# Copies of finished attention results asked for behind all second products of their group

## Chip, cores and metric

The kernel runs on one core of one Trainium2 chip. The metric is the device time of one execution in microseconds (us); the median of three runs before the change is 1055.65 us (1052.11, 1055.65 and 1055.78).

## What is computed

A sigmoid attention over 4 batches and 12 heads, sequence 448, head width 64, followed by two feed-forward layers over the 1792 tokens (widths 768 and 2048), the second with a rational activation. Only the attention is touched:

```python
scores = scale * np.matmul(q, k.transpose(0, 1, 3, 2)) - np.log(S)
attn = 1.0 / (1.0 + np.exp(-scores))
return np.matmul(attn, v)
...
h = x @ w_in;  g = h * sigmoid(h);          x = g @ w_out
h = x @ w_in2; g = P(h) / (Q(h) + 1e-6);  out = g @ w_out2
```

There is no normalisation over the keys, so a result is a plain sum over chunks of keys.

## The kernel before

**Tiling.** Two heads of a batch make a pair; there are 24 pairs (i = 0 to 23). The keys of a pair are cut into chunks of 128, three full ones (c = 0, 1, 2), and the remaining 64 keys of an even pair and of the odd pair behind it share a fourth chunk (c = 3, `LAST`), the even pair's in one half of the partitions and the odd pair's in the other. A **unit** (i, c) is one such chunk, and two pairs make seven units: (e,0) to (e,3), (e+1,0) to (e+1,2). In all there are 84.

**A unit's work.** `attn_QK` (L382) forms the scores on TensorE: three passes (high by high, low key by high query, high key by low query) for two heads, 6 products, or 12 for a shared chunk, where the second six are the next pair's. They go into one of three PSUM buffers called `pair`. `attn_S` (L396) lets ScalarE take the sigmoid from there into SBUF. `attn_AV` (L405) forms the **second products**, sigmoids by values, 4 per unit (8 of half the height for a shared chunk). They add up in `hb`, one PSUM tile of two halves, where even pairs use half 0 and odd pairs half 1. When the last chunk of a pair has been added (the shared one for an even pair, c = 2 for an odd one), `attn_E` copies that half out with VectorE: for the first two batches into `xk` (L420), for the last two into `sb` (L423) with a DMA to DRAM behind it on SyncE's queue (L424).

**Order of the work.** The program's order is written out by hand, and each engine goes through its own part of it in that order. The loop over `groups()` takes three units per turn (the very first three are taken as two and one) and gives, in this order: VectorE's transposition of the queries of a new pair (`attn_X`, L359); the first products of the three units; their sigmoids; TensorE's transposition of the new pair's keys into a `pair` buffer (`attn_T`, L354); the second products of the *previous* turn's three units; and then `attn_C`, which splits the new pair's keys and queries into high and low parts: two ScalarE copies (L365) and two VectorE subtractions (L367), keys first, from the `pair` buffer and from `xq`. Behind that come operand splits for the next layer (`operands0`: L440, L445 and GpSimd's subtractions L482), weight conversions (L237 to L245) and loads.

**Where results get finished.** Six pairs make seven turns (a *block*, four in all), numbered 0 to 6 here. Six of the seven turns finish one pair each, and so copy it once: turns 2 and 3 with the first of their three units, turns 4 and 5 with the second, turns 6 and the next block's 0 with the third. Before the change `attn_E` is called inside `attn_AV`, straight behind the unit that finishes the pair.

```python
for u, p_ in [(u, attn_QK(*u)) for u in units]:
    attn_S(*u, p_)
p = attn_T(new) if new < NPT else None
for u in waiting:
    attn_AV(*u)
waiting = units
if p is not None:
    attn_C(new, *p)
```

**Buffers that matter here.** `pair` is a ring of three: `attn_T` takes the one that the first unit's sigmoid gave back, and the third unit of the next turn gets that same buffer once `attn_C` has read it. `hb` is allocated as one tile, and its two halves are views of it.

Of the kernel before, what the change touches and what calls it, by code (L numbers as in the profile page):

```python
# [47 lines left out]
def attention_moe_moe(ctx: ExitStack, tc: tile.TileContext, q, k, v, w_in1, w_out1, w_in2, w_out2, a, b2, out):  # L48
# [134 lines left out]
    def conv_outs():  # L183
        for do in outs:
            do()
        outs.clear()
# [65 lines left out]
    def conv_rest():  # L252
        for do in halves:
            do()
        halves.clear()
# [15 lines left out]
    def rest_of(i):  # L271
        return HI if i % 2 else LO
# [17 lines left out]
    def load_q(i):  # L290
        if i >= NPT:
            return
        b, hp = divmod(i, NP)
        t = qs[i] = ld_p[0].tile([P, S], F32, tag="qs", name=f"qs_{i}", bufs=3)
        for part in range(2 * D // SQ):
            j, e0 = divmod(part * SQ, D)
            (nc.scalar if i == 0 and part % 2 else nc.sync).dma_start(
                out=t[part * SQ : (part + 1) * SQ, :].rearrange("l (c d) -> l c d", d=SQ),
                in_=q[b, 2 * hp + j, :, e0 : e0 + SQ].rearrange("(c l) d -> l c d", l=SQ),
            )  # L300
# [3 lines left out]
    def mix(i):  # L304
        if i >= NPT:
            return
        t = ks.pop(i)
        u = mixed[i] = ld_p[0].tile([P, 2 * NCH * D], F32, tag="km", name=f"km_{i}", bufs=2)
        dst, src = u.rearrange("p (c h d) -> p h c d", c=NCH, h=2), t.rearrange("p h (c d) -> p h c d", c=NCH)
        if i:  # L310
            nc.gpsimd.tensor_copy(dst, src)
            return
        for h, eng in enumerate((nc.vector, nc.gpsimd)):
            eng.tensor_copy(dst[:, h], src[:, h])
# [34 lines left out]
    def attn_T(i, p=None):  # L349
        t = mixed.pop(i)  # L350
        pk = p if p is not None else pairs.get()
        o = p if p is not None else pk[:, 0, :]
        for c in range(NCH):
            nc.tensor.transpose(o[:, c * P : (c + 1) * P], t[:, c * P : (c + 1) * P], ident)  # L354
        return p, pk, o

    def attn_X(i):
        x = xq[i] = ld_p[0].tile([P, S], F32, tag="xq", name=f"xq_{i}", bufs=1)
        nc.vector.transpose(x, qs.pop(i))  # L359

    def attn_C(i, p, pk, o):
        k_, q_ = st["k", i], st["q", i] = kst.get(), qst.get()
        both = ((k_, o[:, :BK]), (q_, xq.pop(i)))
        for x, src in both:
            nc.scalar.copy(x[:, 0, :], src)  # L365
        for x, src in both:
            nc.vector.tensor_tensor(out=x[:, 1, :], in0=src, in1=x[:, 0, :].bitcast(F32), op=ALU.subtract)  # L367
        if p is None:
            pairs.put(pk)
# [3 lines left out]
    def attn_QK(i, c):  # L373
        p = pairs.get()
        parts = [(i, ((0, 0), (1, 0), (0, 1)))]
        if c == LAST:
            parts.append((i + 1, parts[0][1]))
        turns = [(i_, n) for i_, passes in parts for n in passes]
        for n, (i_, (a_, b_)) in enumerate(turns):
            K, Q = st["k", i_], st["q", i_]  # L380
            for j in range(2):
                nc.tensor.matmul(  # L382
                    p[:, j, :S],
                    K[rows[j], a_, c * P : (c + 1) * P],
                    Q[rows[j], b_, :],
                    start=(n == 0),
                    stop=(n == len(turns) - 1),
                )
        if c == (LAST if i % 2 == 0 else LAST - 1):
            kst.put(st.pop(("k", i)))  # L390
            qst.put(st.pop(("q", i)))
        return p

    def attn_S(i, c, p):
        t = f2.get()
        nc.scalar.activation(t, p[:, :, :S], AF.Sigmoid, bias=nls, scale=QKSCALE)  # L396
        pairs.put(p)
        at[i, c] = t

    def attn_AV(i, c):  # L400
        t = at.pop((i, c))
        for i_ in (i,) if c < LAST else (i, i + 1):
            part = slice(0, P) if c < LAST else rest_of(i_)
            for j in range(2):
                nc.tensor.matmul(  # L405
                    hb[i_ % 2][j * D : (j + 1) * D, :S],
                    vs[i_][part, j, c * D : (c + 1) * D],
                    t[part, j],
                    start=(c == (LAST if i_ % 2 else 0)),
                    stop=(c == (LAST - 1 if i_ % 2 else LAST)),  # L410
                )
        f2.put(t)
        if c == (LAST - 1 if i % 2 else LAST):
            attn_E(i)

    def attn_E(i):
        b, hp = divmod(i, NP)
        del vs[i]
        if b < 2:
            nc.vector.tensor_copy(xk[b * KD + hp], hb[i % 2][:, :S])  # L420
            return
        t = xio.get()
        nc.vector.tensor_copy(t[:, :S], hb[i % 2][:, :S])  # L423
        nc.sync.dma_start(out=xs[0][hp][:, b * S : (b + 1) * S], in_=t[:, :S])  # L424
        xio.put(t)
# [17 lines left out]
    def flush():  # L443
        for src, h, lo in lows:
            nc.vector.tensor_tensor(out=lo, in0=src, in1=h.bitcast(F32), op=ALU.subtract)  # L445
        lows.clear()
# [155 lines left out]
    def prep_ij(g):  # L602
        if g < NGR:
            split_later(wf[g % 2][0], wr[0], wr[1])
# [440 lines left out]
    with tc.manual_schedule():  # L1045
# [33 lines left out]
        def groups():  # L1079
            units = [(i, c) for e in range(0, NPT, 2) for i, c in (*((e, c) for c in range(NCH)), *((e + 1, c) for c in range(LAST)))]  # L1080
            yield (0,), units[:2], 1
            yield (1,), units[2:3], NPT
            at_ = 3
            for e in range(0, NPT, 6):
                n = 2 * e
                for j, (first, size) in enumerate(((0, 2), (2, 1), (3, 2), (5, 2), (7, 1), (8, 2), (10, 2))):
                    if e == 0 and j == 0:
                        continue
                    yield tuple(range(n + first, n + first + size)), units[at_ : at_ + 3], e + 1 + j if j else NPT
                    at_ += 3  # L1090
            assert at_ == len(units)

        begun = 0
        for steps, units, new in groups():
            conv_outs()
            if 0 in steps:
                mix(2)
            for n in steps:
                if n % 2:
                    mix(n // 2 + 3)  # L1100
            if new < NPT:
                attn_X(new)
            for u, p_ in [(u, attn_QK(*u)) for u in units]:
                attn_S(*u, p_)
            p = attn_T(new) if new < NPT else None
            for u in waiting:
                attn_AV(*u)
            waiting = units
            if p is not None:
                attn_C(new, *p)  # L1110
            flush()
            if new < NPT:
                load_q(new + 3)
            conv_rest()
            while begun < (steps[-1] + 1 - 14) * 3 // 4:
                flush()
                next(first_ops, None)
                begun += 1
            for n in steps:
                i, h = divmod(n, 2)  # L1120
                if h == 0:
                    load_k(i + 5)
                at_half = n - 2 * NPT
                if n % 4 == 1:
                    load_v(i + 2)
                    load_v(i + 3)
                if at_half == -8:
                    load_w1(0)
                    load_w1(1)
                if at_half == -5:  # L1130
                    xk_s.close()
                    wr_p, wr_s = opened("wr")
                    wr_p.tile([P, PAD], F32, tag="wrpad", name="wrpad")
                    wr.extend(fixed("wr", 4, [P, DM], F32R, wr_p))
                    wq.extend(fixed("wq", 6, [P, HM], F32R, wr_p))
                    prep_ij(0)
                    sums_12(0)
                if at_half == -3:
                    prep_s12(0)
                if at_half == -1:  # L1140
                    prep_a22(0)
                if n == 0:
                    conv_load()
                if n == 3:
                    conv_load()
                if n == 4:
                    coefficients()
                if n == 12:
                    coefficients_abs()
                if n in CONVS:  # L1150
                    conv(True)
        for _ in first_ops:
            pass
        for u in waiting:
            attn_AV(*u)
        flush()
        bits.put(more_bits)
        ld_s.close()
# [254 lines left out]
        for n in range(HN):  # L1413
# [32 lines left out]
            if n > 3 * HF:  # L1446
                i = n - 3 * HF - 1
# [85 lines left out]
```

## Time and profile before

| what | value |
|---|---|
| median of three runs | 1055.65 us |
| the profiled execution, its own time | 1055.2 us |
| its span in the trace | 1053.4 us |
| TensorE products / weight loads busy | 1028.2 us (98%) / 894.6 us (85%) |
| VectorE, ScalarE, GpSimd busy | 689.3, 653.9, 269.9 us |
| attention, from the first products to the next layer's first | about 7 to 177 us |
| second products L405 | 384, 75.5 us busy, 12.8 us idle ahead of them |

The span is what the trace covers; the time of the execution is 1.8 us longer. "Idle before" is time in which an engine did nothing just ahead of an instruction, with what released it. A product's row is longer than its place in the pipeline, since products overlap; the distance between two starts says what a piece of work costs TensorE. The groups of products in the timeline are merged, so a row "x12" has twelve of them from the start shown.

### The profile page before, as it was taken

Reading aid. Unit: us, or ns where it says so; the run is one execution under the profiler, and the core shown is the slowest. Engines: PE = TensorE matmul, PEld = TensorE weight load, DVE = VectorE, ACT = ScalarE, POOL = GpSimd, SP = SyncE. Lnnn points to the kernel's source line nnn. Section 1 sums busy time; section 2 is a strip of 40 time slices with the busy share of each in tenths; the row PEclk is TensorE's granted clock in tenths of the full one; section 3 lists DMA queues with packets and bytes.
Section 4 is the critical chain, followed back from the end, with each engine's and each line's share of the span. In section 5 each row is a group of like instructions: output and inputs, shape, how many; then the busy total and the mean of one; then the engine's idle time right before and its main releaser. Section 6 shows DMA issues by size and latency. Waiting matters only on the chain.

```text
span 1053.4 us, 15903 instructions
## 1 busy us (share of the span) xinstructions
PE 1028.2 (98%) x5568; PEld 894.6 (85%) x5568; DVE 689.3 (65%) x982; ACT 653.9 (62%) x971; POOL 269.9 (26%) x242
## 2 busy tenths in 40 slices
PE   8999899999999999999999999999999999999998
PEld 5454455899999988899998888888999999999998
DVE  3456544888877748354545628989898977655761
ACT  6677665777676658355545648677777866354430
POOL 4234340000000000000000036579877932310000
PEclk9999999999999999999999999999999999999999
DMA  9866672788777758398979753567678968986641
GB/s 184 184 148 137 143 203 83 249 279 290 247 260 266 268 187 323 106 356 299 369 298 388 307 165 105 200 242 232 218 252 292 314 210 285 333 300 200 206 162 53
DMA packets 182352, 246.15 MB, mean 234 GB/s; under 512 B 57152, under 2 KB 136640, under 8 KB 182272
## 3 DMA queue, kind: packets, MB, share of 16 engines
q1 hardware_dynamic: 168352, 220.95, 64.3%
q10 hardware_dynamic: 11152, 17.36, 4.8%
q0 software_dynamic: 2768, 6.82, 2.7%
q8 instruction: 44, 0.72, 0.3%
q14 instruction: 36, 0.29, 0.1%
HBM read 161.45 MB, written 83.62 MB: 233 GB/s over the span
## 4 chain that ended last, share of the span: by engine, by line
PE 68%; DVE 8%; ACT 2%; DMA 1%; issue 1%; SPq 0%; DVEq 0%; ACTq 0%
PE hp L1000 13%; PE acc L578 10%; PE acc L727 6%; PE acc L725 6%; PE acc L726 6%; PE hb L1000 5%; PE hp L800 5%; PE hp L798 5%; PE hp L799 5%; PE hb L578 4%; PE hb L727 2%; PE hb L726 2%; PE hb L725 2%; DVE sb L831 1%; DVE sb L829 1%
## 5 line engine op out<-in xcount | busy, mean ns | idle before, releaser
L396 ACT ACTIVATE sb<-pair,nls 128x896 f32<-128x896 f32 x84 | 79.2, 1006 | 46.3 <-PE pair L382 46.3
L725 PE MATMUL acc<-xa_all,woH 128*128 128x512 f32 (+1 forms) x252 | 91.9, 365 | 0.0
L726 PE MATMUL acc<-xa_all,woH 128*128 128x512 f32 (+1 forms) x252 | 91.9, 365 | 0.0
L727 PE MATMUL acc<-xa_all,woL 128*128 128x512 f32 (+1 forms) x252 | 91.9, 365 | 0.0
L405 PE MATMUL hb<-sb,vs 128*64 128x448 f32 (+1 forms) x384 | 75.5, 562 | 12.8 <-DVE xk L420 6.0
L435 POOL TENSOR_TENSOR woL<-wif,woH 128x768 fp32r<-128x768 f32 x9 | 16.5, 1855 | 248.1 <-ACT woH L434 248.1
L827 POOL TENSOR_TENSOR sb<-sb 128x1024 f32<-128x1024 f32 (+1 forms) x32 | 69.7, 2179 | 39.0 <-ACT sb L824 39.0
L229 ACT ACTIVATE sb<-sb 128x768 f32<-128x768 f32 x46 | 41.3, 898 | 43.1 <-DMA w1i<-sb 24.8
L578 PE MATMUL acc<-xb,wr 128*128 128x448 f32 x315 | 66.8, 362 | 0.0
L918 POOL TENSOR_TENSOR sb<-sb 128x384 f32<-128x384 f32 (+1 forms) x43 | 52.7, 1231 | 53.1 <-DMA sb<-gk 51.2
L405 PEld LDWEIGHTS hb<-sb,vs 128*64 128x64 f32 (+1 forms) x384 | 19.9, 136 | 52.3 <-issue 27.8
L578 PEld LDWEIGHTS acc<-xb,wr 128*128 128x128 f32 x315 | 59.0, 187 | 4.6 <-issue 0.7
L800 PE MATMUL hp<-hx,woL 128*128 128x512 f32 (+1 forms) x168 | 60.7, 362 | 0.0
L798 PE MATMUL hp<-hx,woH 128*128 128x512 f32 (+1 forms) x168 | 60.7, 362 | 0.0
L799 PE MATMUL hp<-hx,woH 128*128 128x512 f32 (+1 forms) x168 | 60.7, 362 | 0.0
L798 PE MATMUL hp<-xa_all,woH 128*128 128x512 f32 (+1 forms) x168 | 60.7, 362 | 0.0
L799 PE MATMUL hp<-xa_all,woH 128*128 128x512 f32 (+1 forms) x168 | 60.7, 362 | 0.0
L800 PE MATMUL hp<-xa_all,woL 128*128 128x512 f32 (+1 forms) x168 | 60.7, 362 | 0.0
L824 ACT ACTIVATE sb<-sb,absb 128x1024 f32<-128x1024 f32 (+1 forms) x32 | 36.4, 1139 | 33.7 <-DVE hb L845 33.4
L231 DVE TENSOR_SCALAR sb<-sb 128x768 f32<-128x768 f32 x48 | 26.8, 558 | 43.4 <-ACT sb L229 43.2
L230 ACT ACTIVATE sb<-sb,ab 128x768 int32<-128x768 uint16 x54 | 53.6, 993 | 0.0
L829 DVE TENSOR_TENSOR sb<-hp,sb 128x768 f32<-128x768 f32 (+1 forms) x31 | 33.6, 1084 | 28.7 <-ACT sb L826 27.6
(259 smaller groups left out, 2809.8 us busy)
## 6 DMA issues: line engine op xcount, KB each, us to landing
sb<-in_moe_w_out_dram SPq DMA_DIRECT2D x30, 768.0 KB, 6.8
sb<-in_moe_w_in_dram SPq DMA_DIRECT2D x28, 768.0 KB, 7.1
gd<-sb SPq DMA_DIRECT2D x64, 224.0 KB, 2.3
gk<-sb SPq DMA_DIRECT2D x28, 384.0 KB, 3.9
wf<-w0i SPq DMA_DIRECT2D x20, 384.0 KB, 5.5
gk<-sb SPq DMA_DIRECT2D x15, 512.0 KB, 3.4
woL<-gk SPq DMA_DIRECT2D x25, 256.0 KB, 4.7
w1i<-sb SPq DMA_DIRECT2D x16, 384.0 KB, 5.4
```

Source lines behind the costliest of these rows:

```text
L230: nc.scalar.activation(lo, t.bitcast(U16)[:, :, 1], AF.Identity, bias=mid, scale=EIGHTH)
L396: nc.scalar.activation(t, p[:, :, :S], AF.Sigmoid, bias=nls, scale=QKSCALE)
L405: nc.tensor.matmul(hb[i_ % 2][j * D : (j + 1) * D, :S], vs[i_][part, j, c * D : (c + 1) * D], t[part, j], start=(c == (LAST if i_ % 2 else ...
L578: nc.tensor.matmul(o, w_[:, w], x[:, i_, :], start=first and kk == 0 and n_ == 0, stop=kk == HK - 1 and n_ == 2, skip_group_check=not first,)
L725: nc.tensor.matmul(o, woH[c][:, w], x[:, 0, :w_], start=(c == 0), stop=False)
L726: nc.tensor.matmul(o, woH[c][:, w], x[:, 1, :w_], start=False, stop=False)
L727: nc.tensor.matmul(o, woL[c][:, w], x[:, 0, :w_], start=False, stop=(c == KF - 1))
L798: nc.tensor.matmul(o, wh[:, w], x[:, 0, :wd_], start=first, stop=False)
L799: nc.tensor.matmul(o, wh[:, w], x[:, 1, :wd_], start=False, stop=False)
L800: nc.tensor.matmul(o, wl[:, w], x[:, 0, :wd_], start=False, stop=last)
L827: nc.gpsimd.tensor_tensor(out=q_, in0=q_, in1=a_, op=ALU.mult)
L1000: nc.tensor.matmul(o, a_, y[:, w_, :], start=kk_ == 0 and n_ == 0, stop=kk_ == HF - 1 and n_ == 2)
```

## The change

The call of `attn_E` leaves `attn_AV`. A finished pair's number is put on a list, and `full_out()`, called once behind the loop over the waiting units (in the turn, and once more behind the last turn), asks for the copies. Nothing else is edited.

```diff
+    full = []
+
+    def full_out():
+        for i in full:
+            attn_E(i)
+        full.clear()
+
     def attn_AV(i, c):
...
         f2.put(t)
         if c == (LAST - 1 if i % 2 else LAST):
-            attn_E(i)
+            full.append(i)
...
             for u in waiting:
                 attn_AV(*u)
+            full_out()
             waiting = units
...
         for u in waiting:
             attn_AV(*u)
+        full_out()
         flush()
```

**TensorE, turn 2 of the first block** (the 8 second products of the shared unit that finishes pair 0, the first product of the next unit, and the first products of turn 3; vs_317 and vs_322 are the values of pairs 0 and 1, DMASW are loads of values). Before:

```order
L354 MATMUL pair_246<-ident,km_375 128x128 x3
L405 MATMUL hb<-sb,vs_317 64x448 x2
L405 MATMUL hb<-sb,vs_322 64x448 [waits DMASW3_49]
L405 MATMUL hb<-sb,vs_322 64x448
L405 MATMUL hb<-sb,vs_322 64x448 [waits DMASW2_49,DVE_49]
L405 MATMUL hb<-sb,vs_322 64x448 x3
L382 MATMUL pair_244<-qx,xa_all 128x448 [waits Activation_49]
```

And with the change:

```order
L354 MATMUL pair_246<-ident,km_375 128x128 x3
L412 MATMUL hb<-sb,vs_317 64x448 x2
L412 MATMUL hb<-sb,vs_322 64x448 [waits DMASW3_49]
L412 MATMUL hb<-sb,vs_322 64x448
L412 MATMUL hb<-sb,vs_322 64x448 [waits DMASW2_49]
L412 MATMUL hb<-sb,vs_322 64x448 x3
L382 MATMUL pair_244<-qx,xa_all 128x448 [waits Activation_49]
```

The products stand as they did; the first product of the unit behind the finished one no longer waits for VectorE. The same wait goes at sixteen places, turns 2 to 5 of the four blocks.

**TensorE, turn 6 of the last block** (no new pair is transposed any more; vs_1677 are the values of pair 22). Before:

```order
L405 MATMUL hb<-sb,vs_1677 64x448 [waits DMASW7_49,DMASW6_49,DVE_49]
L405 MATMUL hb<-sb,vs_1677 64x448
L382 MATMUL pair_246<-qx,xa_all 128x448 [waits Activation_49]
...
L382 MATMUL pair_245<-qx,xa_all 128x448 x5
L405 MATMUL hb<-sb,vs_1677 64x448 x6
```

And with the change:

```order
L412 MATMUL hb<-sb,vs_1677 64x448 [waits DMASW7_49,DMASW6_49]
L412 MATMUL hb<-sb,vs_1677 64x448
L382 MATMUL pair_246<-qx,xa_all 128x448 [waits Activation_49]
...
L382 MATMUL pair_245<-qx,xa_all 128x448 x5
L412 MATMUL hb<-sb,vs_1677 64x448 [waits DVE_49]
L412 MATMUL hb<-sb,vs_1677 64x448 x5
```

Here the wait on VectorE has moved behind eighteen first products. No other row of any engine differs; VectorE's, ScalarE's, GpSimd's and SyncE's instructions stand in the order that they had.

## Rows read from the trace of the kernel before

**Rows 1.** TensorE's waits in the attention (10 to 178 us): us in total, times, longest.
```profile
PE hb L405 <- DVE xk L420: 6.0, 8, 0.8
```

**Rows 2.** Timeline of TensorE, second block, turns 2 to 5: start us, length us, idle before.
```profile
60.91 0.98 PE L405 MATMUL hb<-sb,vs 64*64 64x448 f32 x8
62.66 1.72 PE L405 MATMUL hb<-sb,vs 128*64 128x448 f32 x8 [0.77 <-DVE xk L420]
64.32 1.48 PE L382 MATMUL pair<-qx,xa_all 64*128 64x448 f32 x12
65.64 1.38 PE L382 MATMUL pair<-xa_all 64*128 64x448 f32 x12
...
67.53 0.97 PE L405 MATMUL hb<-sb,vs 128*64 128x448 f32 x4
...
70.88 2.08 PE L382 MATMUL pair<-xa_all 64*128 64x448 f32 x18
...
73.58 1.89 PE L405 MATMUL hb<-sb,vs 128*64 128x448 f32 x12
...
77.14 2.08 PE L382 MATMUL pair<-xa_all 64*128 64x448 f32 x18
```

**Rows 3.** Timeline of TensorE: second products that no copy interrupts, and what follows them.
```profile
86.39 2.64 PE L405 MATMUL hb<-sb,vs 128*64 128x448 f32 x16
88.96 2.32 PE L382 MATMUL pair<-xa_all 64*128 64x448 f32 x18
91.21 2.48 PE L405 MATMUL hb<-sb,vs 128*64 128x448 f32 x12
93.61 2.68 PE L382 MATMUL pair<-xa_all 64*128 64x448 f32 x24
...
168.90 2.09 PE L382 MATMUL pair<-qx,xa_all 64*128 64x448 f32 x18
170.92 2.64 PE L405 MATMUL hb<-sb,vs 128*64 128x448 f32 x16
```

**Rows 4.** Timeline of VectorE: a copy of turn 2, and turn 6's with the two subtractions.
```profile
61.98 0.62 DVE L420 COPY xk<-hb 128x448 f32<-128x448 f32 x1 [2.67 <-PE hb L405]
...
89.12 0.62 DVE L420 COPY xk<-hb 128x448 f32<-128x448 f32 x1 [1.93 <-PE hb L405]
89.66 0.68 DVE L367 TENSOR_TENSOR xa_all<-pair,xa_all 128x512 fp32r<-128x512 f32 x1
90.26 0.62 DVE L367 TENSOR_TENSOR xa_all<-xq,xa_all 128x448 fp32r<-128x448 f32 x1
```

**Rows 5.** Busy us of each engine by stretch; at the end granted clock, DMA share, GB/s.
```profile
16.00:41.00 25.00, 22.28 (x154) 11.61 (x152) 10.79 (x17) 17.30 (x24) 7.82 (x14) 1.00 0.98 199
...
186.00:230.00 44.00, 42.25 (x211) 38.95 (x210) 36.93 (x61) 34.00 (x58) 0.00 (x0) 1.00 0.82 264
...
330.00:500.00 170.00, 170.00 (x854) 155.52 (x853) 98.11 (x150) 100.33 (x156) 1.09 (x2) 1.00 0.74 255
```

**Rows 6.** Timelines of four engines, third block, turns 5 and 6.
```profile
119.20 2.81 ACT L396 ACTIVATE sb<-pair,nls 128x896 f32<-128x896 f32 x3 [1.22 <-PE pair L382]
...
121.42 1.72 PE L405 MATMUL hb<-sb,vs 128*64 128x448 f32 x8
...
123.19 0.62 DVE L423 COPY sb<-hb 128x448 f32<-128x448 f32 x1 [2.64 <-PE hb L405]
...
125.63 5.00 POOL L482 TENSOR_TENSOR xk<-xk,xk 128x448 f32<-128x448 f32 x3 [10.16 <-DVE xa_all L445]
...
127.38 0.56 ACT L440 CAST xb<-xk 128x448 fp32r<-128x448 f32 x1 [3.97 <-POOL xk L482]
...
129.00 1.08 PE L354 MATMUL pair<-ident,km 128*128 128x128 f32 x4 [2.14 <-ACT sb L396]
```

**Rows 7.** VectorE's subtractions L367: shortest, median, longest ns.
```profile
L367 DVE TENSOR_TENSOR xa_all<-pair,xa_all x23: 680/681/692, 11.0 to 161.9; 128x512 fp32r<-128x512 f32 x23
L367 DVE TENSOR_TENSOR xa_all<-xq,xa_all x16: 615/664/1533, 7.3 to 155.5; 128x448 fp32r<-128x448 f32 x16
```

## The prediction

> **What bounds the kernel now.** I read the stretches first: from 330 to 500 us TensorE is busy for all of 170.00 us, from 186 to 230 us for 42.25 of 44, but from 16 to 41 us, in the attention, only for 22.28 of 25 [rows 5]. The clock granted is 1.00 in these stretches, so it is idle time that is to be looked for. The table of waits names it: second products wait for the copy L420, 8 times and 6.0 us in all, [rows 1], and a row alike stands there for L423, the same copy of the last two batches, with 8 times and 6.0 us too. That makes 16, as many as there are turns 2 to 5 in four blocks. The timeline then shows one such wait: eight second products start at 60.91, the copy runs from 61.98 for 0.62 us, and the next second products start at 62.66, after 0.77 us of an idle TensorE [rows 2, 4]. The copy reads one half of hb, the waiting product writes the other, so it is the tile as a whole that is guarded. Where the finishing unit is the last of its group the row shows no wait: the copy at 89.12 runs beside the first products that started at 88.96 [rows 3, 4].
>
> **What a wait costs.** The 0.77 us is only the visible part, since products overlap and an interrupted pipeline also empties. The distance between two starts shows the whole. Three units of which one is a shared chunk take 2.57 us where nothing interrupts them (86.39 to 88.96), three full chunks 2.40 us (91.21 to 93.61) [rows 3]. With the copy in between:
>
> - Turn 2, shared chunk: 60.91 to 64.32 is 3.41, so 0.84 too much.
> - Turn 3, full chunks: 67.53 to 70.88 is 3.35, so 0.95 too much. Turn 5 is of the same kind, and I give it the same.
> - Turn 4, shared chunk: 73.58 to 77.14 is 3.56, so 0.99 too much [rows 2].
>
> A block loses 0.84 + 0.95 + 0.99 + 0.95 = 3.73 us, four blocks 14.9 us.
>
> **The change part by part.** It adds no instruction and takes none away, and the order of VectorE, ScalarE, GpSimd and SyncE stays. It removes the 16 waits: **-14.9 us**. What it adds is lateness. The copy now comes behind the whole group, and with it everything that is queued behind it on VectorE: the two subtractions that make the low parts of the new pair's keys and queries, then the operand splits. Turns 6 and 0 are the example, since there the copy already came last. With the start of the next first products (88.96) as zero, the copy starts at 0.16, the key subtraction ends at 1.38, the query subtraction at 1.92 [rows 3, 4]. Two things wait for these.
>
> First, the third unit of the next turn needs the pair buffer that the key subtraction reads. The eighteen first products behind turn 6 take 2.25 us (88.96 to 91.21), against 2.02 us (168.90 to 170.92) in the last block, where no new pair is prepared [rows 3]. I put the difference, **0.23 us**, on this wait. It will now also appear behind turns 3, 4 and 5, where the third unit starts at about 1.3; behind turn 2 the second unit is the shared one, with twelve products, and the third comes later than the subtraction.
>
> Second, the low part of the queries. Behind turn 2 the new pair is first used in the second half of the second unit, 65.64 - 64.32 = 1.32 us after the start [rows 2]. At 0.11 us a product, its fifth product, the first with a low query, would start at 1.76, and the low part is there at 1.92: **0.2 us** with the signal. Behind turn 3 the pair is used in the third unit, which by then has already waited for its buffer, so nothing more is due; behind turn 4 in the second half of that unit, later; behind turn 5 two turns later.
>
> So a block pays 0.2 + 3 x 0.23 = 0.89 us. In the last block turn 5 prepares no new pair, which leaves 0.66. Four blocks: 3.3 us. The bounds: nothing, if other work hides it all, and 0.93 us a wait, at which the gain is eaten. I take the middle figures because they are read off the same instructions in turn 6. The wait that moves in the last block's turn 6 stands behind eighteen first products (2.02 us), and the copy is over by 0.16 + 0.62 = 0.78: nothing. The copy's DMA to DRAM goes later by the same amounts; the next layer first reads those rows after the attention, so it is hidden, and the loads behind it on SyncE's queue shift by less than the turns shrink.
>
> One turn is bound by something else. In the third block's turn 6, ScalarE stands for 3.97 us until 127.38 for GpSimd's subtraction, which itself waited for a VectorE split behind the copy; the sigmoids are behind that on ScalarE, and TensorE's transposition waits 2.14 us for one, until 129.00 [rows 6]. Here the copy sets the end. It now starts 1.77 us after its group of second products (121.42 to 123.19) [rows 6]; behind the whole group it would be 2.40 + 0.16 = 2.56, which is 0.79 later. So this event does not give its 0.95 and costs 0.79 on top: **+1.7 us**. The buffer wait of that one turn is inside it, so the 3.3 becomes 3.1.
>
> **Sum.** 14.9 - 3.1 - 1.7 = 10.1 us less. From the profiled execution's 1055.2 us that gives 1045.1, and this execution lies 0.45 us under the median of the three runs. The next layer is paced by its own progress, with TensorE nearly full [rows 5], so I let the gain through to the end. I forecast **1045 us**.
>
> **Rivals.**
>
> *All of it is kept.* If the two late subtractions and the chain of turn 6 are covered after all: 1055.2 - 14.9 = 1040.3 us. For it speaks that each turn gets shorter and so ScalarE, with 1.22 us idle before its sigmoids at 119.20 [rows 6], has less to hide behind; against it, that 0.23 is measured in turn 6. Chance 0.08. The Trainium skill's "PSUM — Partial Sum Buffer", section "PSUM bank collisions raise a hardware error", says that TensorE and VectorE have to be kept apart only within one bank and one group of 32 partitions; by it no copy of one half would have to hold up products into the other, and the chip itself would allow all 14.9. The trace agrees so far that the copy at 89.12 took its usual 0.62 beside products into other buffers [rows 3, 4].
>
> *The subtractions are slowed.* The query subtraction takes 615 ns at best and 1533 at worst, while that from a pair buffer never exceeds 692 [rows 7]. If the later place puts it beside GpSimd's copies and subtractions behind turns 2 and 3, where its end counts, 8 times 0.92 = 7.3 us come back: 1045.1 + 7.3 = 1052.4, within the measurement's grain. Against it: the median is 664, so most places have room. Chance 0.08. The Trainium skill's "SBUF — State Buffer", section "Who interferes with whom", says the same as a rule: a VectorE instruction with two SBUF inputs contends with a GpSimd instruction that reads SBUF. The spread of the one kind and its absence in the other agree [rows 7].
>
> *The loads hold the first block.* DMA is busy for 0.98 of the stretch from 16 to 41 us [rows 5]. If it cannot deliver keys sooner, the first block keeps nothing of its 3.73 - 0.89 = 2.8 us: 1047.9. Chance 0.06.
>
> *Slower: the copy's chain sets the end everywhere.* What happens in the third block's turn 6 happens at all 16 places: the split and conversion work behind the copy on VectorE and GpSimd arrives late at ScalarE, whose queue has the sigmoids behind it. Then each place costs the 0.79 by which the copy is later instead of giving 0.95: 1055.2 + 16 x 0.79 = 1067.8. It decides where ScalarE has to wait for that work ahead of a turn's first sigmoid; before, that is one turn [rows 6], elsewhere ScalarE waits for TensorE, by 1.22 us at 119.20, which is the room there is. Chance 0.05.
>
> *The change does nothing.* The guard of the tile might find another place, in front of the next turn's second products, and time stay at 1055. The order shows the wait gone at 16 places and back at one, where 2 us lie before it. Chance 0.03.
>
> **How the numbers follow.** The forecast has 0.70. A measurement of this kernel can tell about 0.5%, 5.3 us, from no change. Faster by more: the forecast, the full gain and the held first block, 0.70 + 0.08 + 0.06 = 0.84, less 0.02 for a forecast whose unknown costs add up: 0.82. Within: 0.08 + 0.03 + 0.02 = 0.13. Slower: 0.05. The range runs from the full gain, 1040.3, to the slowed subtractions, 1052.4: 1040 to 1053, leaving out the slower case and the one without effect.
>
> **What would show it.** In the changed kernel's profile: no wait of second products for the copy in turns 2 to 5; turns 2 to 5 with second products in 2.4 to 2.6 us; copies 0.16 us after the start of the next first products; waits of TensorE for VectorE's L367 subtraction (a line seven further down) of 0.2 to 0.3 us in their place; and ScalarE's wait for GpSimd in the third block longer by about 0.8 us. The next layer should begin about 10 us earlier. It would be wrong if first products waited over 0.9 us for the subtractions, if ScalarE waited for GpSimd in more than one turn, or if the ten microseconds were there at the attention's end and lost behind it.

## The result, and the profile after

The changed kernel takes 1045.53 us in the median of four runs, against 1054.88 us before. The ratio is 0.9915, with a 95% interval of 0.989 to 0.994: faster by 0.85%, and 0.5 us from the forecast of 1045. The profiled execution took 1046.79 us with a span of 1044.0 us (1055.2 and 1053.4 before).

The table of TensorE's waits in the whole span of the changed kernel (us in total, times, longest):

```profile
PE pair L354 <- ACT sb L396: 3.6, 1, 3.6
...
PE hb L412 <- issue: 0.8, 1, 0.8
```

The sixteen waits for the copies [rows 1] are gone. What is left in the attention is the one stop behind ScalarE in the third block, longer than before (3.6 us, 2.14 in [rows 6]), a wait of 0.8 us at the attention's end, which was there before too, and one of 0.3 us near its start that did not change.

Where the time came from can be read off the distances between starts. Timeline of TensorE in the changed kernel, second block, turns 2 to 5 (start, length, idle before), to be laid beside [rows 2]:

```profile
58.27 2.64 PE L412 MATMUL hb<-sb,vs 64*64 64x448 f32 x16
60.83 1.48 PE L382 MATMUL pair<-qx,xa_all 64*128 64x448 f32 x12
62.15 1.69 PE L382 MATMUL pair<-xa_all 64*128 64x448 f32 x12
...
64.35 2.48 PE L412 MATMUL hb<-sb,vs 128*64 128x448 f32 x12
66.76 2.40 PE L382 MATMUL pair<-xa_all 64*128 64x448 f32 x18
...
69.67 2.79 PE L412 MATMUL hb<-sb,vs 128*64 128x448 f32 x16
72.39 2.27 PE L382 MATMUL pair<-xa_all 64*128 64x448 f32 x18
...
75.80 2.48 PE L412 MATMUL hb<-sb,vs 128*64 128x448 f32 x12
78.20 2.27 PE L382 MATMUL pair<-qx,xa_all 64*128 64x448 f32 x18
...
80.99 2.64 PE L412 MATMUL hb<-sb,vs 128*64 128x448 f32 x16
```

And the rows of before that the comparison needs beyond those shown, timeline of TensorE, turn 5 and the start of turn 6:

```profile
80.34 1.72 PE L405 MATMUL hb<-sb,vs 128*64 128x448 f32 x8
...
83.69 2.10 PE L382 MATMUL pair<-qx,xa_all 64*128 64x448 f32 x18
```

| us, second block | before | after | difference |
|---|---|---|---|
| turn 2, second products | 3.41 | 2.56 | -0.85 |
| turn 3, second products | 3.35 | 2.41 | -0.94 |
| turn 4, second products | 3.56 | 2.72 | -0.84 |
| turn 5, second products | 3.35 | 2.40 | -0.95 |
| turn 3, first products and transposition | 3.21 | 3.52 | +0.31 |
| turn 4, the same | 2.70 | 2.91 | +0.21 |
| turn 5, the same | 3.20 | 3.41 | +0.21 |
| turn 6, the same | 2.70 | 2.79 | +0.09 |

The upper half is the gain, 3.58 us, the lower half what the lateness of the copy costs, 0.82 us; 2.76 us stay in this block. Timeline of VectorE in the changed kernel, turn 2 of that block:

```profile
60.95 0.62 DVE L427 COPY xk<-hb 128x448 f32<-128x448 f32 x1 [4.28 <-PE hb L412]
61.49 0.68 DVE L367 TENSOR_TENSOR xa_all<-pair,xa_all 128x512 fp32r<-128x512 f32 x1
62.09 0.61 DVE L367 TENSOR_TENSOR xa_all<-xq,xa_all 128x448 fp32r<-128x448 f32 x1
```

The copy starts 0.12 us after the first products of turn 3 (60.83), where turn 6 before had 0.16 [rows 4], and the two subtractions follow it. The waits that they cause stand with TensorE's weight loads, which come ahead of the products; the table of products names none. Table of waits of the weight loads in the attention (10 to 168 us), and the one in turn 3:

```profile
PEld pair L382 <- DVE xa_all L367: 4.4, 14, 0.3
```

```profile
62.76 0.71 PEld L382 LDWEIGHTS pair<-xa_all 64*128 64x128 f32 x8 [0.35 <-DVE xa_all L367]
```

Before there were 3 such waits, 1.0 us in all. The load at 62.76 is that of the fifth product in the second half of the second unit, the place that the prediction named; it comes 0.06 us behind the end of the query subtraction (62.09 + 0.61).

The third block is the exception. Timelines of GpSimd, ScalarE and TensorE in the changed kernel, turn 6 there, beside [rows 6]:

```profile
119.08 4.98 POOL L489 TENSOR_TENSOR xk<-xk,xk 128x448 f32<-128x448 f32 x3 [10.27 <-DVE xa_all L452]
```

```profile
120.82 0.56 ACT L447 CAST xb<-xk 128x448 fp32r<-128x448 f32 x1 [4.76 <-POOL xk L489]
```

```profile
116.53 2.27 PE L382 MATMUL pair<-qx,xa_all 64*128 64x448 f32 x18
122.44 0.81 PE L354 MATMUL pair<-ident,km 128*128 128x128 f32 x4 [3.64 <-ACT sb L396]
123.17 4.10 PE L412 MATMUL hb<-sb,vs 128*64 128x448 f32 x16
127.20 2.32 PE L382 MATMUL pair<-xa_all 64*128 64x448 f32 x18
```

ScalarE's wait for GpSimd grew from 3.97 to 4.76 us. The next layer's first product starts at 167.44 us where it started at 176.76. That is 9.3 us, and nothing of it is lost behind: from there to the end of the span it is 876.6 us in both kernels (1053.4 - 176.76 and 1044.0 - 167.44).

### The profile page after: what moved, and what is told of

Same layout as the page of the kernel before. It is cut to its first block, busy times and chain, and to the rows that moved or that the text cites. A ratio compares the mean times of both kernels' runs of the same rounds, so it can differ in the third digit from the quotient of the medians.

```text
span 1044.0 us, 15895 instructions
## 1 busy us (share of the span) xinstructions
PE 1029.8 (99%) x5568; PEld 894.3 (86%) x5568; DVE 687.4 (66%) x982; ACT 654.7 (63%) x971; POOL 268.8 (26%) x242
## 4 chain that ended last, share of the span: by engine, by line
PE 59%; DVE 15%; ACT 4%; issue 2%; DMA 1%; POOL 1%; SPq 0%; DVEq 0%; ACTq 0%
PE hp L1007 14%; PE acc L585 11%; PE acc L734 6%; PE acc L732 6%; PE acc L733 6%; PE hb L1007 5%; PE hb L585 4%; DVE sb L838 3%; DVE sb L836 3%; DVE sb L851 3%; DVE hb L852 2%; ACT sb L833 2%; PE hb L734 2%; PE hb L733 2%; PE hb L732 2%
```

## The experiments

All kernels are compared with the kernel before on the same chip; its median there was 1054.58 us (nine runs) for the first four and 1054.21 us (eleven runs) for the others. The changed kernel's row is that of the section above, against 1054.88 us (four runs). Executions of one kernel differ by up to 4.9 us (e3), so the start of the next layer's first product stands beside each time: it shows what happened in the attention alone, in the one execution that was profiled. From there to the end of the span the ten profiled executions take 875.2 to 877.2 us, so differences of 2 us between medians need not come from the attention.

| kernel | median us | ratio to before, 95% | next layer starts |
|---|---|---|---|
| before | 1054.21 | | 176.76 |
| changed | 1045.53 | 0.9915 (0.989 to 0.994) | 167.44 |
| e1, two tiles, copies early | 1040.41 | 0.9873 (0.9854 to 0.9892) | 162.61 |
| e2, two tiles, copies late | 1042.88 | 0.9892 (0.9875 to 0.9909) | 162.73 |
| e3, copy behind the split | 1040.18 | 0.9867 (0.9846 to 0.9888) | 162.85 |
| e4, splits one step earlier | 1042.55 | 0.989 (0.9874 to 0.9905) | 164.20 |
| e5, turns 2 and 3 only | 1049.4 | 0.9955 (0.9939 to 0.9972) | 172.27 |
| e6, e4 and conversion later | 1041.55 | 0.9881 (0.9865 to 0.9897) | 163.20 |
| e7, e3 and e6 | 1038.09 | 0.9846 (0.9832 to 0.986) | 159.09 |
| e8, e7 with two tiles | 1036.49 | 0.9827 (0.9813 to 0.9841) | 157.87 |

**e1: is it the tile, or the place of the copy?** On the kernel before; the copies stay where they were.

```diff
-        hb_p = ctx.enter_context(tc.tile_pool(name="hbp", bufs=1, space=PSUM))
+        hb_p, hb_s = opened("hbh", space=PSUM)
...
-        hb_all = hb_p.tile([P, 2, 512], F32, tag="hb", name="hb")
-        hb.extend(hb_all[:, j] for j in range(2))
-        hpair.append(hb_all)
+        hb.extend(fixed("hbh", 2, [P, 512], F32, hb_p))
...
         ps_s.close()
+        hb_s.close()
+        hb_p = ctx.enter_context(tc.tile_pool(name="hbp", bufs=1, space=PSUM, reuse_waits="tile"))
+        hb_all = hb_p.tile([P, 2, 512], F32, tag="hb", name="hb")
+        hb[:] = [hb_all[:, j] for j in range(2)]
+        hpair.append(hb_all)
```

> The kernel before, its copies where they were, but the two halves of the result buffer are two tiles (one tile again from the second layer on). My theory: the second products waited because the buffer is guarded as one tile, so the sixteen waits go without any change of order, and nothing becomes late. Gain by the distances of the two traces: 0.84 + 0.94 + 0.84 + 0.94 = 3.56 us a block, 14.2 us in all, less 0.9 for the turn of the third block that the GpSimd chain holds, plus 0.9 for the wait of 0.79 us at the attention's end, which is of the same kind: 14.2 us, about 1040.7 against 1054.9. Rival (the place of the copy in the program is what stalls TensorE): the waits stay and the time is that of the kernel before, 1055.

1040.41 us. Timeline of TensorE, first block, turns 2 and 3, and the last two groups of second products:

```profile
20.05 2.64 PE L405 MATMUL hbh<-sb,vs 64*64 64x448 f32 x16
22.62 1.48 PE L382 MATMUL pair<-qx,xa_all 64*128 64x448 f32 x12
...
25.82 2.48 PE L405 MATMUL hbh<-sb,vs 128*64 128x448 f32 x12
...
157.64 5.04 PE L405 MATMUL hbh<-sb,vs 128*64 128x448 f32 x28
```

Timeline of VectorE, the copy of turn 2 there:

```profile
21.07 0.62 DVE L420 COPY xk<-hbh 128x448 f32<-128x448 f32 x1 [1.98 <-PE hbh L405]
```

The sixteen products run through in 2.57 us although the copy stands ahead of the last eight in the program, and the first products behind them lose nothing: 22.62 to 25.82 is 3.20 us, as before the change. The 28 products at the attention's end have no gap either. The attention ends 14.15 us earlier than before, where 14.2 were expected. So the waits came from guarding two halves as one tile; the place of the copy mattered only through that.

**e2: the late copy with two tiles.** The changed kernel with the edit of e1.

> The changed kernel with two tiles instead of one. My theory: each copy is now released by the last product into its own half and not by the end of the group, so it starts as early as in the kernel before, although it stands behind the group in the program; the time is that of the first experiment, about 1040.7. Rival (a copy that stands later in the program runs later): copies 0.16 us after the start of the next first products and the time of the changed kernel, 1045.5.

1042.88 us; the attention ends at 162.73, 0.12 us from e1. The intervals of the two ratios overlap, and the attention does not explain the 2.5 us between the medians: in the profiled executions what comes behind it differs by 1.5 us (875.7 in e1, 877.2 here). Timeline of VectorE, third block, turn 5:

```profile
113.63 0.62 DVE L430 COPY sb<-hbh 128x448 f32<-128x448 f32 x1 [1.86 <-PE hbh L412]
```

The group's second products start at 111.86, so the copy starts 1.77 us behind them, as it did before the change (121.42 to 123.19, [rows 6]), and not at their end. Asking for the copy late makes it late only where its guard covers the whole group.

**e3: what the lateness costs.** The changed kernel with the copies one step further back.

```diff
-            full_out()
             waiting = units
             if p is not None:
                 attn_C(new, *p)
+            full_out()
```

> The changed kernel with the copies asked for one step later still, behind the split of the new pair (the two subtractions) instead of ahead of it. My theory: in the changed kernel TensorE waits 0.31, 0.22, 0.19 and 0.10 us in turns 3 to 6 because these subtractions stand behind the copy; ahead of it they are done before the group ends, so 0.8 us a block come back (3.2 us), another 0.23 us in each turn 0 (0.8 us), and the chain through GpSimd in the third block starts 1.2 us earlier: 1045.5 - 5.2 = 1040.3. Rival (those waits have another cause, the ring of pair buffers or ScalarE): no wait goes, 1045.5; second rival (the later copy now holds up the next group's second products, which use the same tile): above 1045.5.

1040.18 us. Timeline of VectorE, third block, turn 5:

```profile
112.73 0.69 DVE L367 TENSOR_TENSOR xa_all<-pair,xa_all 128x512 fp32r<-128x512 f32 x1 [1.39 <-ACT xa_all L365]
113.34 0.61 DVE L367 TENSOR_TENSOR xa_all<-xq,xa_all 128x448 fp32r<-128x448 f32 x1
114.17 0.62 DVE L430 COPY sb<-hb 128x448 f32<-128x448 f32 x1 [0.22 <-PE hb L412]
```

The subtractions are over before the group ends (the next first products start at 114.05), and the copy starts where it did in the changed kernel, 0.12 us behind that. The waits of the lower half of the table above go with them: turn 3 of the third block takes 3.22 us from its first products to its second ones (97.41 to 100.63) and turn 4 takes 2.69 (103.03 to 105.72), as before the change. The third block's stop gets shorter, about as expected (1.3 us, 1.2 expected): 5.34 us (114.05 to 119.39) in place of 6.64 (116.53 to 123.17). The attention ends 4.6 us earlier than in the changed kernel; 5.2 were expected. No second products waited for the later copy: the table of waits has none besides the 0.8 us at the attention's end, which were there before.

**e4: the stop in the third block.** The changed kernel with the operand splits begun one step earlier.

```diff
-            while begun < (steps[-1] + 1 - 14) * 3 // 4:
+            while begun < (steps[-1] + 1 - 13) * 3 // 4:
```

> The changed kernel with the operand splits for the next layer begun one step earlier (14 becomes 13 in the rule that counts them), so that the split that GpSimd's subtraction waits for and the split that needs its result fall into different turns. My theory: the stop of TensorE in the third block's turn 6 (6.64 us where 2.79 are normal, and 4.03 us of second products at a lower clock where 2.57 are normal, 5.3 us together) comes from this one chain and goes: 1045.5 - 5.3 = 1040.2. Rival (GpSimd, slowed by the conversions on VectorE, is what holds the turn, and the stop only moves to another one): 1045 within 1 us, with a wait of ScalarE for GpSimd in another turn.

1042.55 us, and 3.2 us in the attention instead of 5.3. The stop is gone, but a smaller one stands in the next turn. Timelines of TensorE, VectorE and GpSimd:

```profile
119.16 0.65 PE L354 MATMUL pair<-ident,km 128*128 128x128 f32 x4
119.74 2.64 PE L412 MATMUL hb<-sb,vs 128*64 128x448 f32 x16
122.31 1.48 PE L382 MATMUL pair<-xa_all 64*128 64x448 f32 x12
125.40 0.88 PE L382 MATMUL pair<-xa_all 64*128 64x448 f32 x6 [1.62 <-DVE xa_all L367]
```

```profile
119.70 2.17 DVE L242 SCALAR_TENSOR_TENSOR sb<-sb 128x768 int32<-128x768 int32 x1
121.91 1.78 DVE L245 SCALAR_TENSOR_TENSOR sb<-sb 128x768 int32<-128x768 int32 x1
123.61 0.63 DVE L359 STREAM_TRANSPOSE xq<-qs 128x448 f32<-128x448 f32 x1
124.17 0.58 DVE L430 COPY sb<-hb 128x448 f32<-128x448 f32 x1
124.68 0.67 DVE L367 TENSOR_TENSOR xa_all<-pair,xa_all 128x512 fp32r<-128x512 f32 x1
```

```profile
120.98 1.89 POOL L489 TENSOR_TENSOR xk<-xk,xk 128x448 f32<-128x448 f32 x1
```

VectorE has no pause here. Two conversions take 2.17 and 1.78 us, behind them stand the transposition of the queries, the copy and the key subtraction, and TensorE's third unit waits for the pair buffer that this subtraction reads. The copy starts 1.86 us behind the next first products (122.31 to 124.17) where 0.12 is usual, and the wait is 1.62 us. ScalarE also waits for the transposition, for 3.06 us, but its copy of the keys was over long before (121.21), so this wait is not on the way. My theory was right about the chain and too generous about what would be free behind it. Of the rival, a part of the stop did move to another turn; the sign that it named, a wait of ScalarE for GpSimd, is not there.

**e5: do the parts add up?** The changed kernel, with copies of a group's second unit made at once.

```diff
-            for u in waiting:
+            for n_, u in enumerate(waiting):
+                held = len(full)
                 attn_AV(*u)
+                if n_ and len(full) > held:
+                    full_out()
             full_out()
```

> The changed kernel, but only a copy of a group's first unit is put off to the end of the group (turns 2 and 3); a copy of the second unit is made straight behind it as before (turns 4 and 5). My theory: each wait has its own price and what it costs in lateness is paid in the next turn, so the parts add up: a block gains 0.84 - 0.31 + 0.94 - 0.22 = 1.25 us, four blocks 5.0 us, and the chain through GpSimd stays as it was before: 1054.6 - 5.0 = 1049.6. The other half, with that chain, is then worth 9.0 - 5.0 = 4.0. Rival (the lateness behind turns 2 and 3 eats their gain, and turns 4 and 5 bring nearly all): above 1053.

1049.4 us. TensorE's waits in the attention:

```profile
PE hb L412 <- DVE xk L427: 3.1, 4, 0.9
PE hb L412 <- DVE sb L430: 3.0, 4, 0.8
```

Eight waits of sixteen are back, and the attention ends 4.5 us earlier than before, where 5.0 were expected and the full change brings 9.3. The other half is then worth 4.8 us, where the expectation had 4.0. So the gain is a sum over the places to within some 0.8 us; e5 leaves open which place the rest belongs to.

**e6: the rest of e4's stop.** e4, and the last conversion begun at step 33.

```diff
-        CONVS = (7, 15, 23, 31)
+        CONVS = (7, 15, 23, 33)
```

> The fourth experiment (operand splits one step earlier), and the last of the four weight conversions of the attention begun at step 33 instead of 31, so that its second half on VectorE no longer runs beside GpSimd's subtractions of the third block's turn 5. My theory: the stop of 1.62 us that the fourth experiment showed in the following turn comes from these two conversion instructions, which took 2.17 and 1.78 us beside GpSimd where they take 0.95 elsewhere and held up the transposition of the queries behind them; it goes, and the time is 1042.6 - 1.7 = 1040.9. Rival (GpSimd's subtractions themselves are too late for the splits): a stop of the same size stays, 1042.6.

1041.55 us; the attention ends 1.0 us earlier than in e4. Timelines of TensorE and VectorE, third block, turns 5 and 6:

```profile
124.41 0.88 PE L382 MATMUL pair<-xa_all 64*128 64x448 f32 x6 [0.66 <-DVE xa_all L367]
```

```profile
118.84 1.56 DVE L452 TENSOR_TENSOR xb<-xk,xb 128x448 fp32r<-128x448 f32 x1
120.33 0.96 DVE L238 TENSOR_SCALAR sb<-sb 128x768 f32<-128x768 f32 x1
121.32 1.37 DVE L239 TENSOR_SCALAR sb<-sb 128x768 int32<-128x768 int32 x1
...
123.17 0.58 DVE L430 COPY sb<-hb 128x448 f32<-128x448 f32 x1
```

The stop shrank from 1.62 to 0.66 us, and with it the lateness of the copy, from 1.86 us behind the next first products to 0.90 (122.27 to 123.17). The conversion's second half left the turn, but its first half came into it, and with the split ahead of it these three now take 3.89 us together where elsewhere they take 0.62, 0.55 and 0.56 (62.62 to 63.74 us in the changed kernel's second block). That VectorE's work of this turn holds up the copy and the key subtraction behind it is shown by both halves. That GpSimd's work beside it makes it long is read from the two running at the same time; no run took GpSimd's work away, and which of its instructions slows which was not told apart.

**e7 and e8: all of it.** e7 is e3 with the edits of e4 and e6; e8 is e7 with the two tiles of e1.

> The third experiment (copy behind the split of the new pair) with the edits of e6 (operand splits one step earlier, conversion at step 33). If the parts are independent, the third experiment's 1040.2 loses the stop of turn 6 in the third block, which in it is 5.34 + 4.20 us where 2.69 + 2.57 are normal, 4.3 us: 1035.9. Rival (the stop moves to another turn, as it did in part in the fourth experiment): 1038 to 1040.

> e7 with the result buffer as two tiles. It should in addition lose the wait of 0.79 us between the last two groups of second products, 0.95 us with the emptied pipeline, since these add to the other half: 1035.0. Rival (the copy already stands where nothing waits for it): as e7.

1038.09 and 1036.49 us, 2.2 and 1.5 us above what was expected. The stop is gone in both. Timeline of TensorE in e7, third block, turn 6:

```profile
114.56 2.10 PE L382 MATMUL pair<-qx,xa_all 64*128 64x448 f32 x18
116.70 0.63 PE L354 MATMUL pair<-ident,km 128*128 128x128 f32 x4
117.26 2.64 PE L412 MATMUL hb<-sb,vs 128*64 128x448 f32 x16
119.83 2.07 PE L382 MATMUL pair<-xa_all 64*128 64x448 f32 x18
```

2.70 and 2.57 us in place of 5.34 and 4.20 in e3: 4.3 us, as reckoned. The attention ends 3.8 us earlier than in e3, so that 0.5 us went elsewhere in it (one wait of 0.20 us for the query subtraction in turn 2 is new); the rest of the difference lies outside it, perhaps in the median of e3 that I reckoned from, whose four runs lie between 1037.64 and 1042.52. e8 ends the attention 1.2 us before e7, where 0.95 was expected: 0.87 us of it because nothing waits between the last two groups (4.97 us from 152.90 in place of 5.84 from 153.25), the other 0.35 before these. e8 is the fastest kernel here, 1.7% below the kernel before and about 9 us below the changed one.

## Why the prediction was right

**The bound and the waits.** Right. The sixteen waits were the kernel's to lose, they went at the sixteen places, and nothing before or behind the attention took the gain back. e1 shows the reason given for them: with two tiles they go without any change of order. The Trainium skill's "PSUM — Partial Sum Buffer", section "PSUM bank collisions raise a hardware error", would allow a copy beside products into another bank, and e1 agrees: there copies of one half run beside products into the other and take 0.62 us as ever. The guard was the tile's, not the chip's.

**The gain, 14.9 us.** A little too large, by a mis-sized term: 0.99 us for turn 4. I took 2.57 us for its uninterrupted group from turn 6, where the shared chunk comes last. In the middle of a group, as in turn 4, the same products take 2.72 us in this kernel and 2.71 in e1 (30.92 to 33.63), so the wait was worth 0.84. That is 0.15 us a block, 0.6 in all.

**The lateness, 3.3 us less 0.2.** Right in sum, 0.82 us a block against 0.89, with its shares shifted: 0.31 behind turn 2 where I had 0.2, 0.09 behind turn 5 where I had 0.23. Why it is less behind turn 5 was not tried. The cause is shown by e3, which takes the subtractions from behind the copy and loses all four, and by the weight loads, which name the subtraction as what they waited for.

**The chain of the third block, 1.7 us.** Right: the block keeps 1.09 us (96.61 to 129.46 after, 102.01 to 135.95 before, the two starts of second products that bound it) where the second keeps 2.76, so 1.67 went there, and ScalarE's wait grew by 0.79 us, the figure by which the copy was reckoned later. e4 shows that it hangs on the splits falling into one turn. One thing was not in the sum: none of the stretches in [rows 5] covers the time behind this stop, where the granted clock is 0.50 (from 129 to 132 us in the kernel before). It did no harm only because it comes out even. Against before, the second products behind the stop take 0.33 us longer (4.03 and 3.70) and the transposition 0.28 us less (0.73 and 1.01). That is luck.

**The sum.** 10.1 us foretold, 9.3 measured in the attention and 9.35 between the medians. Of the missing 0.8 us 0.6 are turn 4's, and 0.1 was lost ahead of the first of the sixteen places (the second products there start at 19.95 in place of 19.84 us); the rest I did not trace. That the time came as close as 0.5 us has some luck in it: a gain too large by 0.75 us was taken from a start 0.3 us too high (the profiled execution's 1055.2, with a median of 1054.88).

**The rivals.** The full gain did not come, because the lateness is real (e3). The slowed subtractions came once: behind the second block's turn 5 the query subtraction took 1.76 us, at a place where its end does not count. The loads did not hold the first block, which kept 2.75 us (30.27 to 27.52 from its turn 2 to the second block's turn 0). The chain that sets the end everywhere stayed in its one turn.

## What to carry to other kernels

Where one engine writes one half of a buffer and another reads the other half, look at how the buffer is declared before reordering: here two tiles (e1) gave half as much again as the reordering, and the same copy put behind the split instead of ahead of it (e3), so that nothing else became late with it, gave as much as two tiles. Price a wait by the distance between two starts, against the same work in the same order uninterrupted: the idle time shown (0.73 to 0.77 us) was 0.07 to 0.22 us less than what came back, and the same work in another order (2.57 for 2.72) off by 0.15.

## What the runs showed of the hardware

**The one long stop also halved TensorE's clock.** Table of stretches of the changed kernel in the third block (busy us of each engine; at the end granted clock, DMA share, GB/s):

```profile
119.00:122.40 3.40, 0.00 (x0) 0.00 (x0) 3.37 (x3) 1.58 (x3) 3.24 (x2) 1.00 0.60 118
122.40:124.00 1.60, 1.56 (x8) 0.76 (x10) 1.23 (x2) 1.60 (x3) 1.60 (x2) 0.61 0.91 287
124.00:125.00 1.00, 1.00 (x6) 0.44 (x4) 0.00 (x0) 1.00 (x4) 1.00 (x3) 0.50 0.72 169
125.00:126.00 1.00, 1.00 (x4) 0.00 (x0) 0.00 (x0) 0.49 (x2) 1.00 (x3) 0.50 0.98 343
126.00:127.20 1.20, 1.20 (x10) 0.21 (x8) 0.00 (x0) 0.00 (x0) 1.20 (x3) 0.93 1.18 360
```

After 3.6 us without work the granted clock fell to 0.50, 1.2 of 2.4 GHz, and came back only near the group's end, so that its second products took 4.03 us (123.17 to 127.20) instead of 2.57: the stop cost 3.85 us itself and 1.46 more behind it. The kernel before shows the same behind its stop of 2.14 us: its second products there take 3.70 us (130.01 to 133.71). The sixteen waits of 0.73 to 0.77 us left the clock at 1.00 (from 60 to 124 us in the kernel before). A kernel that loses the one long stop (e4) has a mean clock of 1.000 in its profile where the changed one has 0.998, and its second products take 2.57 us (119.74 to 122.31). Other executions may differ: of the twenty of the kernel before that stand beside the experiments, nine have a mean clock of 0.998 (1053.69 to 1056.05 us) and eleven 0.999 or 1.000 (1052.34 to 1054.66), while all four of the changed kernel have 0.997 or 0.998. Where in those runs the clock was low is not on record.

**VectorE's conversions beside GpSimd.** The two instructions L242 and L245 took 0.95 and 0.96 us in one turn of the changed kernel (89.40 and 90.39 us) and 2.17 and 1.78 in e4's third block (119.70 to 123.69), where GpSimd issues DMAs until 120.43 us and then copies and subtracts until 122.87 beside them. The Trainium skill's "SBUF — State Buffer", section "Who interferes with whom", has it that a VectorE instruction with two SBUF inputs contends with a GpSimd instruction that reads SBUF; the rows agree, by a factor of about two here. Other rows show that this is not the whole of it: L242 took its 0.95 us at 118.85 in the changed kernel too, though a subtraction began beside it at 119.08, and L238 and L239, which have one input, took 0.96 and 1.37 us in e6 where they take 0.55 and 0.56 elsewhere. I had priced such a slowing for the query subtraction alone; that conversions ahead of the copy and the key subtraction could pass it on to TensorE I had not seen.
